# Sparse attention into a swish block on one core: key tiles moved by 16 tokens, attention tiled by head pair, long-run float32 loads, crossbar transposes, the first batch in halves, and every engine in written order

## The chip, the core and the metric

The kernel runs on one core of a Trainium2 chip (trn2). The engines are named as the profile names them: PE multiplies matrices (PEld is its weight load), DVE and ACT work on vectors, POOL does so too and issues its own DMAs, and SP only issues DMAs and waits. The metric is the time of one execution in device microseconds (us); lower is better. Several executions are timed, and one more is profiled.

## The reference

For each of 4 batches and 8 heads (768 tokens, head width 64) the kernel computes attention over two kinds of keys, and the result of all heads goes through a two-layer block.

```python
k_sum = k.reshape(B, H, nb, block, D).max(axis=3)      # 24 blocks of 32 tokens
v_sum = v.reshape(B, H, nb, block, D).mean(axis=3)
scores_l = scale * q @ k^T, kept where |i - j| < 16    # else -1e9
scores_s = scale * q @ k_sum^T + log(block)
a = softmax(concat(scores_l, scores_s))
attn = a @ concat(v, v_sum)
x = attn as (B*S, H*D)                                 # 3072 x 512
h = x @ w_in                                           # 512 x 2048
g = h * sigmoid(beta * h)
out = g @ w_out                                        # 2048 x 512
```

Inputs and output are float32. Both kernels multiply in bfloat16 and accumulate in float32.

## The kernel before

**Attention.** A query tile has 64 tokens, so a sequence has 12 of them. A query tile needs the keys from 15 tokens before it to 15 after it, and the 24 block maxima. Keys and queries of two heads (a pair, `g`, four per batch) lie on 128 partitions, 64 per head. One key tile of 128 columns holds 64 + 32 keys, 24 block maxima and padding. Even and odd query tiles (`par`) have different layouts: `kw` has a copy for each. A query operand `q2` holds the two heads side by side with zeros in the other head's rows, so that one matmul of 128 rows and 128 columns gives the scores of both heads (`scores`, L244, matmuls L259). ACT takes the exponential (L261). In batch 0 the mask is added by a matmul (L254); in the others DVE multiplies by a band of zeros and ones (L264). `av` (L267) multiplies by values that carry a column of ones, so that the sum of the weights comes out as well (L276); DVE takes the reciprocal (L278) and scales (L281).

**Preparation.** POOL loads and casts keys, queries and values (`load` L76, `casts` L184). PE transposes keys and queries (`prep_qk` L208, matmuls L215 and L235), DVE and ACT copy them out of PSUM. `prep_v` (L191) forms the block means by six matmuls, and four small SP transfers place value rows and means. `x_transpose` (L286) turns the attention result on PE. In batch 0 the loads are float32 and go through SP's and ACT's queues; later ones go through POOL's queue and are cast on the way.

**The block.** `h_tile` (L301) makes 128 of the 2048 hidden rows for 768 tokens: eight matmuls of 384 columns into one PSUM tile of two banks, and one ACT instruction on both banks (L309). `o_part` (L314) makes a fourth of one 128-token output block: four matmuls of 512 columns; after the fourth part DVE copies the block to SBUF (L324) and SP stores it (L325). Two output blocks share one PSUM tile, a bank each; the pool has three such tiles, and scores, attention results, hidden rows and outputs draw from it in turn.

**Order.** `merge` (L327) interleaves the preparation of the next batch with the `h_tile`s of this one, and the next batch's scores and `av`s with this batch's `o_part`s. SP and POOL run in written order (L25); PE, DVE and ACT are ordered by the scheduler of the language. The weights are loaded by POOL's queue, `w_in` and `w_out` in four pieces each (L342, L345), behind the casts of batch 0. `w_out` is divided by `beta` in place (L170).

Of the kernel before, what the change touches and what calls it, by code (L numbers as in the profile page):

```python
# [11 lines left out]
def kernel(  # L13
# [11 lines left out]
    ctx.enter_context(tc.manual_schedule(engines={mybir.EngineType.SP, mybir.EngineType.Pool}))  # L25
# [4 lines left out]
    ACTF = mybir.ActivationFunctionType  # L30

# [5 lines left out]
    nch = S // P  # L37
    NE = 2
    NF = S // NE
    nc3 = NF // P  # L40
    npair = H // 2
# [4 lines left out]
    n_tokens = B * S  # L46
    k1 = d_model // P
    k2 = d_ff // P
    VW = 2 * D + 1
    NEG = -30000.0  # L50


    SUM = (QT + W, W)
    assert d_model == H * D and out.shape == (n_tokens, d_model)

    const = ctx.enter_context(tc.tile_pool(name="consts", bufs=1))
    wpool = ctx.enter_context(tc.tile_pool(name="weights", bufs=1))
    qk_pool = ctx.enter_context(tc.tile_pool(name="qk", bufs=4))
    st_pool = ctx.enter_context(tc.tile_pool(name="st", bufs=9))
    at_pool = ctx.enter_context(tc.tile_pool(name="attn", bufs=4))  # L60
    x_pool = ctx.enter_context(tc.tile_pool(name="x", bufs=3))
    xt_pool = ctx.enter_context(tc.tile_pool(name="xt", bufs=2))
    moe_pool = ctx.enter_context(tc.tile_pool(name="moe", bufs=2))
    ps = ctx.enter_context(tc.tile_pool(name="ps", bufs=1, space=bass.MemoryType.PSUM))

    q_r, k_r = (a.rearrange("b (g h) (c p e) d -> b g p (h c) (e d)", p=P, h=2, e=NE) for a in (q, k))
    v_r = v.rearrange("b (g h) (c p) d -> b g p (h c) d", p=P, h=2)
    out_r = out.rearrange("(a p) d -> a p d", p=P)
    srcs = {"v": v_r, "k": k_r, "q": q_r}
    FE = 2 * S * D // P  # L70


    staged = {}
    hold = [moe_pool.tile([P, 4, FE], f32, name=f"hold{i}", tag="h_sb", bufs=4) for i in range(3)]

    def load(nm, b, g, eng):  # L76
        if b == 0:
            i = ("k", "q", "v").index(nm)
            f = hold[i][:, g]
        else:  # L80
            f = st_pool.tile([P, FE], bf16, name="st", tag="st")[:]
        dst = f.rearrange("p (n d) -> p n d", d=D if nm == "v" else NE * D)
        eng.dma_start(out=dst, in_=srcs[nm][b, g])  # L83
        staged[(nm, b, g)] = f

    load("k", 0, 0, nc.sync)
    load("q", 0, 0, nc.scalar)
    load("v", 0, 0, nc.sync)
    load("k", 0, 1, nc.scalar)
    load("q", 0, 1, nc.sync)  # L90
    load("v", 0, 1, nc.scalar)


    identity = const.tile([P, P], bf16, name="identity")
    make_identity(nc, identity)
    identity32 = const.tile([P, P], f32, name="identity32")
    nc.vector.tensor_copy(out=identity32[:], in_=identity[:])
# [5 lines left out]
    A_avg = const.tile([P, nch, P], bf16, name="A_avg")  # L103
    nc.vector.memset(A_avg, 0.0)
    nc.vector.memset(A_avg[:, :, 0:nb], 1.0 / block)
    select(A_avg[:, :, 0:nb], 0, [[P, nch], [-block, nb]], 1)
    select(A_avg[:, :, 0:nb], block - 1, [[-P, nch], [block, nb]], -1)

    band = const.tile([P, 2, QT], bf16, name="band")
    negband = const.tile([P, 2, QT], bf16, name="negband")  # L110
    bias = const.tile([P, 2], f32, name="bias")
    for par in range(2):
        near, far, summ = (const.tile([P, QT], bf16, name=f"{nm}{par}") for nm in ("near", "far", "summ"))
        nc.vector.memset(near, 1.0)
        nc.vector.memset(far, 1.0)
        nc.vector.memset(summ, 1.0)
        o = QT * par
        select(near, W - 1 - o, [[-1, QT]], 1)
        select(near, W - 1 + o, [[1, QT]], -1)
        if par == 0:  # L120
            select(far, -(P - W) - 1, [[-1, QT]], 1)
        else:
            select(far, -(QT - W) - 1, [[1, QT]], -1)
        select(summ, -SUM[par], [[0, QT]], 1)
        select(summ, SUM[par] + nb - 1, [[0, QT]], -1)
        nc.vector.tensor_add(out=near, in0=near, in1=far)

        nc.vector.tensor_add(out=band[:, par], in0=near, in1=summ)
        nc.vector.tensor_scalar(out=negband[:, par], in0=band[:, par], scalar1=1.0, scalar2=-NEG,  # L129
                                op0=ALU.subtract, op1=ALU.mult)  # L130
        nc.vector.tensor_scalar(out=bias[:, par:par + 1], in0=summ[:, 0:1], scalar1=log_block,
                                scalar2=None, op0=ALU.mult)

    NKW = 4
    kw_bufs = [const.tile([P, 2, nch, P], bf16, name=f"kw{i}") for i in range(NKW)]
    q2_bufs = [const.tile([P, nch, 2, 2, QT], bf16, name=f"q2{i}") for i in range(NKW)]

    ve_bufs = [const.tile([P, npair, nch + 1, VW], bf16, name=f"ve{i}") for i in range(2)]
    vo_bufs = [const.tile([P, npair, nch + 1, VW], bf16, name=f"vo{i}") for i in range(2)]

    def clear_qk(i):
        nc.vector.memset(q2_bufs[i][0:D, :, :, 1, :], 0.0)
        nc.vector.memset(q2_bufs[i][D:P, :, :, 0, :], 0.0)
        for par in range(2):
            nc.vector.memset(kw_bufs[i][:, par, :, SUM[par] + nb:SUM[par] + 2 * W], 0.0)
        nc.vector.memset(kw_bufs[i][:, 0, 0, P - W:P], 0.0)
        nc.vector.memset(kw_bufs[i][:, 1, nch - 1, 0:W], 0.0)

    def clear_v(i):
        nc.vector.memset(ve_bufs[i][:, :, 0:nch, 2 * D:VW], 1.0)  # L150
        nc.vector.memset(ve_bufs[i][:, :, nch], 0.0)
        nc.vector.memset(vo_bufs[i][:, :, 1:, 2 * D:VW], 1.0)
        nc.vector.memset(vo_bufs[i][:, :, 0], 0.0)

    clear_qk(0)
    clear_v(0)

    w_in_sb = wpool.tile([P, k1, d_ff], bf16, name="w_in_sb")
    w_out_sb = wpool.tile([P, k2, d_model], bf16, name="w_out_sb")
    beta_sb = wpool.tile([P, k2], f32, name="beta_sb")  # L160
    inv_beta = wpool.tile([P, k2], f32, name="inv_beta")
    beta_tmp = wpool.tile([k2, P], f32, name="beta_tmp")

    def load_beta():
        beta_ps = ps.tile([P, k2], f32, name="beta_ps", tag="t", bufs=2)
        nc.tensor.transpose(beta_ps[:], beta_tmp[:], identity32[:k2, :k2])
        nc.vector.tensor_copy(out=beta_sb[:], in_=beta_ps[:])
        nc.vector.reciprocal(out=inv_beta[:], in_=beta_sb[:])

    def scale_w_out(n):  # L170
        nc.vector.tensor_scalar(out=w_out_sb[:, n], in0=w_out_sb[:, n], scalar1=inv_beta[:, n:n + 1],
                                scalar2=None, op0=ALU.mult)

    last = {}

    def cast_qk(nm, b, g):
        t = qk_pool.tile([P, nc3, NE, 2, D], bf16, name=nm + "_nat", tag=nm + "_nat")
        f = staged.pop((nm, b, g)).rearrange("p (h c e d) -> p c e h d", h=2, e=NE, d=D)
        last["cast"] = nc.gpsimd.tensor_copy(out=t[:], in_=f)  # L179
        return t  # L180
# [3 lines left out]
    def casts(b, g):  # L184
        nat[(b, g)] = cast_qk("k", b, g), cast_qk("q", b, g)
        ve, vo = ve_bufs[b % 2][:, g], vo_bufs[b % 2][:, g]
        f = staged.pop(("v", b, g)).rearrange("p (h c d) -> p c h d", h=2, d=D)
        nc.gpsimd.tensor_copy(out=ve[:, 0:nch, 0:2 * D].rearrange("p c (h d) -> p c h d", h=2), in_=f)
        nc.gpsimd.tensor_copy(out=vo[:, 1:, 0:2 * D].rearrange("p c (h d) -> p c h d", h=2), in_=f)

    def prep_v(b, g):  # L191
        ve, vo = ve_bufs[b % 2][:, g], vo_bufs[b % 2][:, g]
        vm_ps = ps.tile([P, 2 * D], f32, name="vm_ps", tag="t", bufs=2)
        for c in range(nch):
            nc.tensor.matmul(vm_ps[:], A_avg[:, c, :], ve[:, c, 0:2 * D], start=(c == 0), stop=(c == nch - 1))  # L195
        vm = x_pool.tile([nb, 2 * D], bf16, name="vm", tag="vm")
        nc.vector.tensor_copy(out=vm[:], in_=vm_ps[0:nb])
        nc.sync.dma_start(out=vo[0:W, 1:], in_=ve[0:W, 1:])
        nc.sync.dma_start(out=ve[P - W:P, 0:nch], in_=vo[P - W:P, 0:nch])
        src = vm[:, None].to_broadcast([nb, nch, 2 * D])  # L200
        nc.sync.dma_start(out=ve[SUM[0]:SUM[0] + nb, 0:nch, 0:2 * D], in_=src)
        nc.sync.dma_start(out=vo[SUM[1]:SUM[1] + nb, 1:, 0:2 * D], in_=src)

    xT = {}
    x_nat = {}
    at = {}

# [157 lines left out]
    for g in range(npair):  # L365
        casts(0, g)
        if g == 2:
            load_w_in(0)
# [87 lines left out]
```

## Time and profile before

| | us |
|---|---|
| three timed executions | 260.85, 263.31, 315.06 (median 263.31) |
| span of the profiled execution, first to last instruction | 261.8 |
| PE busy in the span | 228.0 (87%) |
| DVE, ACT, POOL busy | 153.3, 115.6, 93.3 |
| hidden rows, 512 matmuls of 384 columns | 91.1 busy |
| outputs, 384 matmuls of 512 columns | 92.0 busy |
| exponentials and hidden-row activations on ACT | 28.2 and 57.5 |
| first hidden-row matmul; first unbroken stretch of them | at 43.8; from 50.6 |
| batch starts after it, by the chain | 103.6, 157.7, 211.7 |

The profile's page is that of one execution. No separate time of that execution is listed: its span is 1.5 us below the median of the timed ones. A row of a group reads: line, engine, operation, what is written from what is read, shape and count, then busy time, the mean time of one in ns, and the idle time before. Busy time of PE counts the overlap of matmuls that follow each other once, while the mean of one includes its way through the array: matmuls of 384 columns take 333 ns each by the row, and 16 of them in a row pass in 2.60 us, 162 ns each.

### The profile page before, as it was taken

What the parts mean: (1) busy time and instruction counts of PE and PEld (TensorE: products, weight loads), DVE (VectorE), ACT (ScalarE), POOL (GpSimd) and SP (SyncE); (2) the same over time, 40 slices, a digit from 0 to 9 for tenths busy, and PEclk for the clock granted to TensorE, in tenths of its full rate; (3) what the DMA queues carried; (4) which work ended last, traced back from release to release, by engine and by line L of the source; (5) the groups of instructions that cost most, each with busy time, mean ns of one, the idle gap of its engine ahead of it and who ended that gap; (6) DMA issues with size and microseconds to landing.
All of it is one profiled execution on the core that took longest, in us unless ns stands there. A gap on an engine that the chain in (4) does not pass through costs nothing.

```text
span 261.8 us, 4353 instructions
## 1 busy us (share of the span) xinstructions
PE 228.0 (87%) x1681; PEld 138.1 (53%) x1681; DVE 153.3 (59%) x355; ACT 115.6 (44%) x136; POOL 93.3 (36%) x126
## 2 busy tenths in 40 slices
PE   0473866599999879999999999999999999999984
PEld 0262643266665545566665555666655545654431
DVE  7672775669668888266658792666688831001221
ACT  1355641376684320476782331677833306661000
POOL 6679522599999990199510000000000000000000
PEclk9997695789999999999999999999999999999999
DMA  7999999999899999279401111101011111001111
GB/s 180 264 262 148 192 206 201 163 106 112 88 141 148 119 112 155 82 72 119 49 18 74 49 40 62 31 24 25 21 40 71 52 43 40 0 0 43 73 54 73
DMA packets 63667, 24.53 MB, mean 94 GB/s; under 512 B 49808, under 2 KB 60576, under 8 KB 63648
## 3 DMA queue, kind: packets, MB, share of 16 engines
q0 software_dynamic: 41664, 11.28, 42.8%
q1 hardware_dynamic: 18864, 11.82, 16.6%
q10 hardware_dynamic: 3120, 1.18, 2.0%
q8 instruction: 13, 0.21, 0.3%
q14 instruction: 6, 0.05, 0.1%
HBM read 27.27 MB, written 6.29 MB: 128 GB/s over the span
## 4 chain that ended last, share of the span: by engine, by line
PE 68%; DMA 12%; DVE 9%; POOL 5%; SPq 2%; issue 2%; ACT 1%; POOLq 0%; ACTq 0%
PE h_ps L307 32%; PE o_ps L320 25%; DMA st<-in_k_dram 8%; DVE x_nat L281 4%; DMA hold_86<-in_v_dram 4%; DVE attn L264 3%; PE s_ps L259 2%; SPq L83 2%; PE px L292 2%; PE av_ps L276 2%; PE pk L215 2%; PE vm_ps L195 2%; PE pq L235 2%; ACT attn L261 1%; POOL w_in_sb L343 1%
## 5 line engine op out<-in xcount | busy, mean ns | idle before, releaser
L320 PE MATMUL o_ps<-w_out_sb,h_sb 128*128 128x512 bf16 x384 | 92.0, 379 | 0.8 <-DVE o_sb L324 0.8
L307 PE MATMUL h_ps<-xT,w_in_sb 128*128 128x384 bf16 x512 | 91.1, 333 | 0.0
L309 ACT ACTIVATE h_sb<-h_ps,beta_sb 128x768 bf16<-128x768 f32 x64 | 57.5, 900 | 49.8 <-PE h_ps L307 48.9
L307 PEld LDWEIGHTS <-w_in_sb 128*128 128x128 bf16 x512 | 49.8, 99 | 31.6 <-issue 2.0
L320 PEld LDWEIGHTS <-h_sb 128*128 128x128 bf16 x384 | 35.9, 98 | 35.1 <-issue 1.5
L324 DVE COPY o_sb<-o_ps 128x512 f32<-128x512 f32 x24 | 16.6, 690 | 48.7 <-PE o_ps L320 48.4
L261 ACT ACTIVATE attn<-s_ps,bias 128x768 bf16<-128x768 f32 x32 | 28.2, 900 | 34.7 <-PE s_ps L259 26.9
L281 DVE TENSOR_TENSOR x_nat<-av_ps,r 64x384 bf16<-64x384 f32 x64 | 35.5, 555 | 1.5
L276 PEld LDWEIGHTS <-attn 128*128 128x128 bf16 x192 | 14.2, 103 | 16.9 <-issue 6.2
L264 DVE TENSOR_TENSOR attn<-attn,band 128x768 bf16<-128x768 bf16 x24 | 16.1, 671 | 9.9 <-ACT attn L261 9.6
L179 POOL COPY k_nat<-st 128x768 bf16<-128x768 bf16 x12 | 10.9, 908 | 21.5 <-PE pk L215 16.4
L227 DVE TENSOR_REDUCE km<-pk 128x24 bf16<-128x768 bf16 x16 | 15.2, 950 | 5.2 <-ACT kw_139 L225 1.7
L83 POOL DMA_DIRECT2D st<-in_v_dram x12 | 12.5, 1040 | 5.5 <-DMA w_in_sb<-in_moe_w_in_dram 3.2
L215 PEld LDWEIGHTS <-k_nat 128*128 128x128 bf16 x96 | 7.7, 110 | 11.1 <-issue 6.0
L254 PE MATMUL s_ps<-negband,identity 128*128 128x384 bf16 x16 | 6.5, 422 | 7.2 <-DVE negband L129 7.0
L276 PE MATMUL av_ps<-ve_146,attn 128*128 128x129 bf16 x48 | 4.9, 242 | 9.0 <-DMA ve_146<-vm 9.0
L278 DVE RECIPROCAL r<-av_ps 128x6 f32<-128x6 f32 x32 | 6.2, 194 | 10.9 <-PE av_ps L276 10.4
L215 PE MATMUL pk<-identity,k_nat 128*128 128x128 bf16 x96 | 9.3, 239 | 3.1 <-POOL k_nat L179 3.1
L292 PE MATMUL px<-identity,x_nat 128*128 128x128 bf16 x96 | 8.8, 232 | 3.3 <-DVE x_nat L281 2.9
L83 POOL DMA_DIRECT2D st<-in_q_dram x12 | 10.0, 837 | 2.7 <-DMA w_out_sb<-in_moe_w_out_dram 1.8
L235 PE MATMUL pq<-identity,q_nat 128*128 128x128 bf16 x96 | 9.0, 236 | 2.2 <-POOL q_nat L179 1.7
L292 PEld LDWEIGHTS <-x_nat 128*128 128x128 bf16 x96 | 5.9, 103 | 9.4 <-DVE x_nat L281 9.4
(136 smaller groups left out, 240.9 us busy)
## 6 DMA issues: line engine op xcount, KB each, us to landing
out_dram<-o_sb SPq DMA_DIRECT2D x24, 256.0 KB
st<-in_k_dram POOLq DMA_DIRECT2D x12, 192.0 KB, 3.9
st<-in_q_dram POOLq DMA_DIRECT2D x12, 192.0 KB, 4.9
st<-in_v_dram POOLq DMA_DIRECT2D x12, 192.0 KB, 5.7
w_in_sb<-in_moe_w_in_dram POOLq DMA_DIRECT2D x4, 512.0 KB, 8.2
w_out_sb<-in_moe_w_out_dram POOLq DMA_DIRECT2D x4, 512.0 KB, 17.5
hold_84<-in_k_dram SPq DMA_DIRECT2D x3, 384.0 KB
hold_86<-in_v_dram SPq DMA_DIRECT2D x3, 384.0 KB
```

The lines of the kernel that those rows point to most:

```text
L83: eng.dma_start(out=dst, in_=srcs[nm][b, g])
L215: nc.tensor.transpose(pk[:, e, c * P:(c + 1) * P], kt[:, c, e], identity)
L227: nc.vector.tensor_reduce(out=km[:], in_=pk.rearrange("p e (n f) -> p n e f", f=block // NE), op=ALU.max, axis=mybir.AxisListType.XY)
L261: nc.scalar.activation(out=a.rearrange("p (k j) h q -> p k (j h q)", k=2), in_=big[:, :, 0:w], func=ACTF.Exp, bias=bias[:, par:par + 1], s ...
L264: nc.vector.tensor_mul(out=a, in0=a, in1=band[:, par, None, None, :].to_broadcast([P, nch, 2, QT]))
L276: nc.tensor.matmul(ov[:, m // TB, m % TB], a[:, m], vt[:, m], start=True, stop=True)
L281: last["norm"] = nc.vector.tensor_mul(out=x[par * QT:(par + 1) * QT, :, hh, :].rearrange("p (k j) d -> p k j d", k=2), in0=ov[lo:lo + D, : ...
L292: nc.tensor.transpose(px[:, c * P:(c + 1) * P], x[:, c], identity)
L307: nc.tensor.matmul(big[:, kk, 0:MG], w_in_sb[:, ki, ni * P:(ni + 1) * P], xT[b][:, ki, kk * MG:(kk + 1) * MG], start=(ki == 0), stop=(ki = ...
L309: nc.scalar.activation(out=h_bufs[(b, ni // 8)][:, ni % 8, :].rearrange("p (k m) -> p k m", k=2), in_=big[:, :, 0:MG], func=ACTF.Silu, sca ...
L320: nc.tensor.matmul(o_ps, h_bufs[(b, ni // 8)][:, ni % 8, ms * P:(ms + 1) * P], w_out_sb[:, ni, :], start=(ni == 0), stop=(ni == k2 - 1))
L324: nc.vector.tensor_copy(out=o_sb[:], in_=o_ps)
```

## The change

Nearly every line of the kernel is written anew. Names and lines from here on are the new ones where they differ.

- **All engines in written order.** The scheduler places nothing any more; `run` and `put` write each side task behind a numbered main task. Four PSUM tiles of two banks each (`big[0]` to `big[3]`) are named by hand and stay for the whole kernel.
- **Key tiles moved by 16 tokens.** One layout for all 12 query tiles: 96 keys, 24 maxima, 8 zeros. The values get the matching layout: the tile `ve` starts 16 tokens early and has 13 tiles for two heads, `vo` is `ve` moved by 64 rows. The mask is the same for every tile but the first and last.
- **Attention per head and pair.** A scores matmul has 64 rows (one head) and 64 columns; the two heads use the two halves of the array's rows and the two banks of a tile. In `av` the weights are the 64 columns of one query tile, 65 value columns pass, and the result lands in one half of the partitions. DVE scales both heads of a pair in one instruction.
- **Loads.** Keys and queries come as float32 in runs of 2 KB (1 KB for the first batch's queries, which come in halves) on 96 partitions, values in runs of 256 bytes. All go through SP's queue. `w_in` stays on POOL's queue; `w_out` comes as float32 through SP's queue in eight pieces and is cast and divided by `beta` on DVE.
- **Transposes.** In batch 0 keys and queries are transposed on PE in float32 by matmuls with an identity (`kt0`, `qt0`), the attention result on PE in bfloat16. In batches 1 to 3 all three are transposed by DMAs on SP's queue (`kq_dma`, `x_dma`), after a cast on DVE (keys) or POOL (queries).
- **Batch 0 in halves.** Scores, `av` and the result are made for tokens 0 to 383 first and then for 384 to 767; the hidden rows likewise, in two passes of 16 `h_half`s, each followed by its own ACT instruction.
- **Outputs.** `o_atom` puts all output blocks of a batch into `big[0]`, the banks in turn; the first three blocks of batch 0 run side by side (`o3`), the last block of all is cut in two.

The core of the new code:

```diff
-    ctx.enter_context(tc.manual_schedule(engines={mybir.EngineType.SP, mybir.EngineType.Pool}))
+    ctx.enter_context(tc.manual_schedule())
+    big = [ps.tile([P, 2, 512], f32, name=f"big{i}") for i in range(4)]
...
+    def kt0(g):
+        t = big[g % 2].rearrange("p k (c f) -> p (k c) f", f=P)[:, :, 0:R]
+        f = stg[("k", 0, g)][0:R].rearrange("p (h c d) -> p h c d", h=2, d=D)
+        for c in range(8):
+            for h in range(2):
+                nc.tensor.matmul(t[h * D:(h + 1) * D, c], f[:, h, c], identity32[0:R, 0:R], start=True, stop=True)
+        windows(act_cp, g, t)
+        key_max(g, t)
+        key_sums(nc.gpsimd, g)
...
+        for j in range(HT):
+            m = u * HT + j
+            for h in range(2):
+                lo = h * D
+                nc.tensor.matmul(s[:, h, j * QT:(j + 1) * QT], kw[g][lo:lo + D, m, :], q_tile(b, g, h, m),
+                                 start=not on_pe, stop=not on_pe or j == HT - 1)
...
+    def v_odd_dma(g):
+        nc.sync.dma_start(out=vo[0:QT, g, :, :], in_=ve[QT:P, g, :, :])
+        nc.sync.dma_start(out=vo[QT:NK, g, 0:JV - 1, :], in_=ve[0:2 * W, g, 1:JV, :])
...
+    def vm_all(bg, bank):
+        t = big[bg][:, bank].rearrange("p (h g d) -> p h g d", h=2, g=G)
+        for h in range(2):
+            for j in range(J6 + 1):
+                nc.tensor.matmul(t[:, h], A[:, j], ve[:, :, h * J6 + j, 0:D], start=(j == 0), stop=(j == J6))
+        r = slice(NK, NK + nb)
+        nc.vector.tensor_copy(out=vm_sb[r], in_=t[r])
...
+                    nc.tensor.matmul(tv[par * QT:(par + 1) * QT, j, h], e[:, h, lo:lo + QT],
+                                     (vo if par else ve)[:, g, h * J6 + J, 0:D + 1], start=True, stop=True)
...
+    def x_dma(b, g):
+        nc.sync.dma_start_transpose(out=xT[:, g, :].rearrange("p (j t) -> p j t", j=J6),
+                                    in_=xn[(b, g)].rearrange("p j h d -> p (j h d)"))
...
+    def kq_dma(nm, b, g):
+        t = (kT if nm == "k" else qT)[g]
+        nc.sync.dma_start_transpose(out=t[:], in_=nat[(nm, b, g)][0:R].rearrange("p c h d -> p (c h d)"))
...
+    def h_half(i, kk, t):
+        lo = kk * HS
+        for ki in range(k1):
+            nc.tensor.matmul(t[:, 0:HS], w_in_sb[:, ki, i * P:(i + 1) * P], xT[:, ki, lo:lo + HS],
+                             start=(ki == 0), stop=(ki == k1 - 1))
+        nc.scalar.activation(out=h_sb[:, i, lo:lo + HS], in_=t[:, 0:HS], func=ACTF.Silu, scale=beta_sb[:, i:i + 1])
...
+    def o_atom(b, ms, a):
+        t = big[0][:, ms % 2]
+        for n in range(4 * a, 4 * a + 4):
+            o_mm(ms, n, t)
+        if a == 3:
+            o_out(b, ms, t)
...
+    banks = [big[3][:, 0], big[3][:, 1], big[0][:, 0], big[0][:, 1], big[1][:, 0], big[1][:, 1]]
...
+    run([lambda i=i: h_half(i, 0, banks[i % 6]) for i in range(k2)], sides)
...
+            put(sides, 0, lambda n=n: [load_k(n, g, nc.sync) for g in range(G)],
+                lambda n=n: [load_q(n, g, nc.sync) for g in range(G)])
+            for g in range(G):
+                put(sides, 2 + g, lambda g=g: kq_cast(nc.vector, "k", n, g), lambda g=g: kq_dma("k", n, g))
+            put(sides, 5, lambda n=n: [load_v(n, g, nc.sync) for g in range(G)])
+            for g in range(G):
+                put(sides, 4 + g, lambda g=g: windows(pool_cp, g, kT[g][:]), lambda g=g: key_max(g, kT[g][:]),
+                    lambda g=g: key_sums(nc.vector, g))
+                put(sides, 6 + g, lambda g=g: kq_cast(nc.gpsimd, "q", n, g), lambda g=g: kq_dma("q", n, g))
+                put(sides, 11 + g, lambda g=g: v_cast(nc.gpsimd, g), lambda g=g: v_odd_dma(g))
+            put(sides, 15, lambda: vm_all(3, 0))
+        run([lambda i=i: h_tile(i) for i in range(k2)], sides)
+        sides = {}
+        if n < B:
+            attention(n, sides, [0, 1, 4, 5, 6, 7, 8, 9], 7, 2, None)
+            put(sides, 2, lambda: vm_spread(nc.vector, vo), lambda: vm_spread(nc.vector, ve))
+        main = [lambda ms=ms, a=a: o_atom(b, ms, a) for ms in range(J6 - (n == B)) for a in range(4)]
+        run(main, sides)
```

`windows` copies the 96 keys of each of the 12 tiles into `kw` (three copies), `key_max` takes the 24 maxima, `key_sums` writes them into the tiles, `v_cast` casts values into `ve`, `vm_spread` copies the block means into `ve` or `vo` (two copies each), and `attention` writes the scores and `av`s of the next batch behind the numbered output parts. `qt0` is `kt0` for four of eight columns of the queries, with one copy out of PSUM by DVE.

## The prediction

> **What bounds the kernel now.** I read the page's busy rows and slices first, then the chain in order of time, then the groups for durations.
>
> ```profile
> PE 228.0 (87%) x1681; PEld 138.1 (53%) x1681; DVE 153.3 (59%) x355; ACT 115.6 (44%) x136; POOL 93.3 (36%) x126
> PE   0473866599999879999999999999999999999984
> PE 68%; DMA 12%; DVE 9%; POOL 5%; SPq 2%; issue 2%; ACT 1%; POOLq 0%; ACTq 0%
> ```
>
> PE is full from slice 8 on (6.5 us each) and leads the chain: after the first 50 us the kernel is a queue of matmuls. The chain in order of time shows what one costs:
>
> ```profile
> 109.95 0.34 PE pq L235 x6
> 110.28 2.60 PE h_ps L307 x16
> 112.88 0.35 PE vm_ps L195 x6
> 236.08 17.44 PE o_ps L320 x80
> 253.54 0.70 DVE o_sb L324
> 254.29 3.63 PE o_ps L320 x16
> ```
>
> A matmul of 384 columns passes in 2.60/16 = 0.162 us, one of 512 in 17.44/80 = 0.216 (218 by the row), one of 128 with its own weights in 0.34/6 = 0.057. So the block costs 512 x 0.162 + 384 x 0.216 = 166 us in any order. The last three lines show a price that the change pays often: the sixth output block uses the other bank of the PSUM tile that the fifth has just filled, and PE stands from 253.54 to 254.29, until DVE has copied the first bank. Elsewhere the scheduler puts other matmuls there (the page gives L320 0.8 us of idle in all).
>
> ```profile
> L309 ACT ACTIVATE h_sb<-h_ps,beta_sb 128x768 bf16<-128x768 f32 x64 | 57.5, 900 | 49.8 <-PE h_ps L307 48.9
> L179 POOL COPY k_nat<-st 128x768 bf16<-128x768 bf16 x12 | 10.9, 908 | 21.5 <-PE pk L215 16.4
> st<-in_k_dram POOLq DMA_DIRECT2D x12, 192.0 KB, 3.9
> ```
>
> These give ACT's time for two banks, POOL's for 768 elements (829 to 908 ns, 1.1 ns an element), and 3.9 us from issue to landing for a pair's keys. By form:
>
> ```profile
> L166 PE MATMUL beta_ps<-identity_98,beta_tmp 16*128 16x16 f32 x1 | 0.2, 231 | 0.0
> L230 DVE COPY kw_139<-km 128x144 bf16<-128x144 bf16 x8 | 4.1, 599 | 0.1
> L230 DVE COPY kw_141<-km 128x144 bf16<-128x144 bf16 x8 | 1.4, 223 | 0.1
> ```
>
> **What the change does to PE's work.** Before, 768 short matmuls: 192 scores, 192 `av`, 288 transposes, 96 for block means. After, 384 scores and 384 `av`: 768 again, with 64 or 65 columns instead of 128. A weight load still stands before each, so I price them at 0.055, near the 0.057 row. Bounds: 0.028 (half the columns), 0.1 (the 97 to 109 ns of a weight load, unhidden). So crossbar transposes take 4 us a batch off PE and finer attention puts 5 us on. No gain here.
>
> [...]
>
> **Same-tile waits.** In the built program the first matmul into the second bank of a tile waits for the reader of the first. `h_half` fills a bank with four matmuls (0.65), ACT reads it, and only then comes the other bank: ACT's 384 columns take about 0.55 (between half of 0.900 and 0.6), with 0.17 to leave the array (333 less 162 ns) and 0.08 of signals 0.8. Nothing can fill the gap, since the order is written. `o_atom` uses `big[0]` for all blocks, so each block pays what 253.54 to 254.29 shows, with the drain 0.95.
>
> **Stage by stage**, following each engine's written order with these durations:
>
> *Until the first hidden-row matmul: 51* (before 43.8, and 50.6 until unbroken). The first keys land near 3.5 (first long load before: 5.07 - 0.81 with two queues sharing). Then PE runs all 128 float32 transposes, since the second halves of queries and scores stand ahead of the first `h_half` too. The nearest float32 row is 231 ns at 16 columns; the nearest transposes take 57. I take 0.2, so 25.6. Scores and masks 7.4, `av` and means 4. POOL's chain of a pair (cast 0.9, four moves 1.1, weight issue 0.8) is 2.8 us against 1.4 of PE work, leaving 7 uncovered over four pairs; one PSUM bank waits for DVE's copies, 3. Sum 51; bounds 39 (0.057) and 58 (0.231, slow clock at the start). The halves thus bring little: only the second `av`s lie beside hidden rows.
>
> *Two passes of `h_half`: 43.* Each 16 x 0.65 = 10.4 and 8 x 0.8 = 6.4; the first also has four `av`s with their waits for DVE (4 x 1.1) and ACT's table load of 1.3 (sum 22); the second ends 4 us early for the weights (21).
>
> *Why the weights are late.* SP's order is keys, queries, four key transposes, one query transpose, then half of `w_out`. The key casts stand on DVE behind the first pass, and each next cast behind the maximum of the keys just transposed. A crossbar transpose is in no row: between 1.95 (an output store, issue to landing) and 5.7 (the value loads of the page); I take 3.5, near the keys' 3.9. A link is cast 0.9, transpose 3.5, maximum 0.95: 5.4, and four end when the second pass does. The eight `w_out` loads follow, then the values.
>
> *Outputs of batch 0: 47.* 20.7 + 192 x 0.055 = 10.6 + means 1.5, and waits: weights 4 + 4 + 2, two boundaries 2, `av` behind DVE's spread and scaling 5 (sum 50; I take 47, since the last waits overlap). Before: 28.
>
> *Hidden rows of batches 1 and 2: 31 each* (before, with preparation, 28). 20.8, the 14 matmuls of `vm_all` 3 (256 columns each, at half speed, as the trace's six L276 matmuls at 40.95 take 0.81 after a stall and 0.35 otherwise), and a stall of 7 at them. They need all four value casts, which stand on POOL behind four `windows` (1120 elements, 1.4 us) and four query casts (1.15): 5.5 + 4.6 + 3.7 = 14 us that begin only when the first keys are transposed, 10 us in, because that transpose stands on SP behind eight loads of 384 KB.
>
> *Outputs of batches 1 and 2: 40 each* (before 26). 20.7 + 10.6, then DVE's four `vm_spread` copies of 1536 elements ahead of the first output copy: at 0.9 each (the 144 broadcast elements of L230 in 223 ns give up to 2.4 if time goes by elements, and at least 0.22) and the mask products beside them 5 us of stall; two open boundaries 2, other waits 1.7.
>
> *Batch 3: 20.8 + 27.* 20.7, four boundaries 3.8, last copy and store 2.5.
>
> 51 + 43 + 47 + 31 + 40 + 31 + 40 + 48 = 331. This is against the profiled span of 261.8; the median of the timed runs is 1.5 above it, which I leave in the rounding: **330**.
>
> [...]
>
> **Rivals.**
>
> 1. *PE never waits* (the other side; place: both banks' borders, output borders, means). If hidden and output rows of the two banks flow without the waits and preparation is always ahead, the stalls above go: 13 in `h_half`, 16 + 8 + 8 + 4 at outputs, 7 + 7 at the means, 10 in the head: 73 less, 257, 2% under the time before. For: DVE at 59% and ACT at 44% have room. Against: the waits are in the program, and one stands in this trace at 253.54. It decides from 68 of the 73 on. Chance 0.04.
> 2. *Cheap transposes and short matmuls.* Float32 at 0.057 and short ones at 0.028: 12 less in the head, 15 in three output stages: 300 to 310. For: two heads use different rows of the array. Against: separate weight loads. Chance 0.22.
> 3. *The crossbar is the bound.* At 5.7 us or more a transpose, four links of the key chain add 9, each hidden stage 3, the borders of batches 3: 350 to 368. [...] Against: 192 KB is what one of the page's loads moves. Chance 0.24.
> 4. *The first batch is not in halves in effect*: counted above, since the halves do not shorten the head. Were all its second-half work to slide beside the first pass, the head would be 15 shorter: 315. It lies inside the forecast's band.
>
> Forecast 330 (312 to 348): chance 0.5.
>
> **Range.** The unknown prices give 300 (float32 0.057, short 0.028, transposes 1.95) to 368 (5.7, spread copies at 2.4); I leave 0.1 on each side: 300 to 368. A run can tell 2% from no change. Slower by over 2%: 0.96; within: 0.02; faster: 0.02, from rival 1, which lies on the border.
>
> **What would show it.** PE idle before `h_half` released by ACT, 16 times some 0.8; before `o_atom` released by DVE's output copy; before `vm_all` by POOL's value casts; the first output rows by the weights' scaling on DVE; the first hidden matmul near 51; periods of some 71 us instead of 54. Wrong if hidden rows begin under 40, the periods are under 62, or the transposes take over 6 us each.

## The result and the profile after

The changed kernel takes **340.62 us** (median of four executions, 337.52 to 341.82), the kernel before 263.26 beside it. The ratio is 1.294, 95% interval 1.283 to 1.305; here and below a ratio leaves out executions over 1.5% above the fastest of their kernel (of the kernel before the one at 315.06), a median does not, and none is given where a single execution would be left. In a later group the changed kernel took 340.89 (337.34 to 343.17). The profiled execution took 341.82, its span is 339.8.

First the page of the changed kernel: busy rows, slices (8.5 us each), granted clock, and the shares of the chain that ended last.

```profile
PE 254.5 (75%) x2057; PEld 141.6 (42%) x2075; DVE 129.3 (38%) x223; ACT 109.7 (32%) x144; POOL 73.0 (21%) x113
PE   4685677866386797599566997997046997999885
PEclk9995587999785799989858799999559899999999
PE 48%; DMA 18%; DVE 15%; ACT 7%; SPq 6%; issue 4%; POOL 2%; POOLq 0%; DVEq 0%; ACTq 0%
```

No engine but PE is busy for half the span, and PE is not full either. Its idle time is 339.8 - 254.5 = 85.3 us, against 261.8 - 228.0 = 33.8 before: 51.5 of the 78 us. The other 26.5 are more busy time. Of that, 6.5 is the output matmuls, the same work at a lower granted clock (0.85 to 0.91 in the outputs of batches 0 to 2, where the kernel before had 0.97 to 1.00 from 50.6 on; 98.5 us busy against 92.0; 18 of its 400 records are missing here, and the second profile of the changed kernel, which has them all, gives 101.7). The hidden rows took 64.9 + 25.5 = 90.4 against 91.1. The rest of PE's work, attention and transposes, went from 228.0 - 92.0 - 91.1 = 44.9 to 254.5 - 98.5 - 90.4 = 65.6; a part of that, some 8 us by an estimate from starts, is changes between matmuls that use different rows or columns of the array (last section).

Now the same execution cut at the first matmul of each stage. Columns: stretch, its length, busy time of PE, PEld, DVE, ACT and POOL with instructions, PE's granted clock, DMA share and GB/s.

```profile
0.00:48.70 48.70, 32.95 (x485) 25.61 (x485) 22.10 (x67) 15.71 (x28) 20.85 (x53) 0.79 0.94 199
48.70:92.70 44.00, 27.87 (x197) 13.99 (x189) 17.01 (x31) 21.12 (x36) 14.02 (x16) 0.92 0.23 59
92.70:139.00 46.30, 37.15 (x296) 18.20 (x303) 22.34 (x41) 9.87 (x11) 4.39 (x5) 0.85 0.64 167
139.00:175.90 36.90, 25.91 (x144) 15.08 (x143) 16.46 (x13) 14.42 (x16) 16.93 (x20) 0.84 0.90 193
175.90:214.60 38.70, 32.85 (x285) 15.57 (x289) 14.99 (x26) 9.87 (x11) 0.00 (x0) 0.89 0.26 64
214.60:253.40 38.80, 23.86 (x143) 14.52 (x142) 16.37 (x13) 14.42 (x16) 16.83 (x20) 0.82 0.90 177
253.40:290.70 37.30, 31.62 (x285) 15.33 (x288) 14.98 (x26) 9.87 (x11) 0.00 (x0) 0.91 0.31 67
290.70:311.50 20.80, 20.80 (x129) 12.53 (x128) 0.69 (x1) 13.52 (x15) 0.00 (x0) 1.00 0.04 13
311.50:339.80 28.30, 21.50 (x112) 10.81 (x111) 4.31 (x7) 0.90 (x1) 0.00 (x0) 0.97 0.15 56
```

Every stage that prepares a next batch is long and at a clock of 0.82 to 0.92; the last batch has nothing to prepare and runs at 0.97 to 1.00. Set beside the kernel before, by its batch starts:

| from, to | before, us | after, us |
|---|---|---|
| start to the hidden rows of batch 1 | 103.6 | 139.0 |
| batch 1 | 54.1 | 75.6 |
| batch 2 | 54.0 | 76.1 |
| batch 3 | 50.1 | 49.1 |

Where PE stands is told by the view of waits, PE's rows of the changed kernel. Columns: who waits for whom, us in total, how often, the longest.

```profile
PE big L310 <- POOL ve L278: 22.3, 2, 14.9
PE big L390 <- DVE o_sb L395: 12.8, 12, 2.9
PE big L390 <- DVE w_out_sb L193: 10.6, 3, 5.1
PE big L373 <- ACT h_sb L375: 10.4, 16, 2.3
PE big L233 <- DMA stg<-in_k_dram: 4.5, 1, 4.5
```

The first four rows are 56 us: block means waiting for value casts, outputs for the copy of the block before or for scaled weights, half rows for ACT. PE's timeline shows the two same-tile waits (columns: start, length, what, and in brackets the idle time before it and its releaser):

```profile
71.83 1.46 PE L373 MATMUL big<-xT,w_in_sb 128*128 128x384 bf16 x8 [0.67 <-ACT h_sb L375]
...
320.39 3.61 PE L390 MATMUL big<-w_out_sb,h_sb 128*128 128x512 bf16 x16 [0.78 <-DVE o_sb L395]
```

Eight matmuls, two half rows, then 0.67 of nothing; and 0.78 between two output blocks of the last batch.

The chain in order of time, ahead of the block means of batch 3, shows how the longest kind of wait comes about:

```profile
216.36 4.36 DMA stg<-in_k_dram
220.72 12.74 DMA kT<-kn
...
248.78 1.66 POOL ve L278 x2
...
250.49 3.14 PE big L310 x14
```

The first key transpose is issued at 220.72 and lands 12.74 later, at 233.45: it stands behind eight loads of 384 KB. POOL copies keys from there on without a break, value casts last, and PE's means begin at 250.49.

### The profile page after: what moved, and what is told of

The parts are those of the page before. It is cut to its first block, busy times and chain, and to the rows that moved or that the text cites. A ratio compares the mean times of both kernels' runs of the same rounds, so it can differ in the third digit from the quotient of the medians.

```text
span 339.8 us, 5101 instructions
## 1 busy us (share of the span) xinstructions
PE 254.5 (75%) x2057; PEld 141.6 (42%) x2075; DVE 129.3 (38%) x223; ACT 109.7 (32%) x144; POOL 73.0 (21%) x113
## 4 chain that ended last, share of the span: by engine, by line
PE 48%; DMA 18%; DVE 15%; ACT 7%; SPq 6%; issue 4%; POOL 2%; POOLq 0%; DVEq 0%; ACTq 0%
PE big L390 24%; DMA kT<-kn 9%; PE big L383 6%; PE big L267 5%; ACT e L271 3%; PE big L373 3%; DVE o_sb L395 3%; DMA stg<-in_k_dram 3%; DMA vst<-in_v_dram 3%; DVE km L213 2%; PE big L243 2%; PE big L310 2%; PE big L332 2%; DMA beta_tmp<-in_moe_beta_dram 2%; DVE xn L343 2%
## 5 line engine op out<-in xcount | busy, mean ns | idle before, releaser
L390 PE MATMUL big<-w_out_sb,h_sb 128*128 128x512 bf16 (+1 forms) x382 | 98.5, 400 | 26.4 <-DVE o_sb L395 12.8
L390 PEld LDWEIGHTS <-h_sb 128*128 128x128 bf16 x400 | 39.2, 103 | 72.2 <-issue 35.9
L383 PE MATMUL big<-xT,w_in_sb 128*128 128x384 bf16 x384 | 64.9, 332 | 3.7 <-DMA xT<-xn 3.7
L385 ACT ACTIVATE h_sb<-big,beta_sb 128x768 bf16<-128x768 f32 x48 | 43.2, 901 | 67.0 <-PE big L383 67.0
L226 POOL COPY kw<-kT 128x80 bf16<-128x80 bf16 (+1 forms) x36 | 30.2, 880 | 140.8 <-DMA kT<-kn 135.3
L271 ACT ACTIVATE e<-big,bias 128x768 bf16<-128x768 f32 x32 | 28.4, 901 | 50.7 <-PE big L267 50.7
L373 PE MATMUL big<-xT,w_in_sb 128*128 128x384 bf16 x128 | 25.5, 338 | 10.4 <-ACT h_sb L375 10.4
L273 DVE TENSOR_TENSOR e<-e,mask 128x768 bf16<-128x768 bf16 x24 | 13.4, 558 | 43.9 <-ACT e L271 43.8
L213 DVE TENSOR_REDUCE km<-kT 128x24 bf16<-128x768 bf16 x12 | 17.5, 1455 | 27.6 <-DMA kT<-kn 27.6
L310 PE MATMUL big<-ve,A_avg 128*128 128x256 bf16 x42 | 8.0, 367 | 22.3 <-POOL ve L278 22.3
L375 ACT ACTIVATE h_sb<-big,beta_sb 128x384 bf16<-128x384 f32 x32 | 18.6, 581 | 18.3 <-PE big L373 17.6
L267 PE MATMUL big<-qT,kw 64*128 64x64 bf16 x288 | 19.6, 281 | 0.0
L217 DVE COPY kw<-km 128x288 bf16<-128x288 bf16 x12 | 16.8, 1401 | 0.4
L343 DVE TENSOR_TENSOR xn<-big,r 128x768 bf16<-128x768 f32 (+1 forms) x20 | 15.9, 797 | 0.7
L310 PEld LDWEIGHTS <-A_avg 128*128 128x128 bf16 x42 | 5.3, 126 | 24.8 <-issue 22.7
```

The costliest lines, as they stand in the source:

```text
L213: nc.vector.tensor_reduce(out=km[g][:], in_=src.rearrange("p c (n f) -> p n f c", f=4), op=ALU.max, axis=AX.XY)
L226: nc.gpsimd.tensor_copy(out=o, in_=i)
L267: nc.tensor.matmul(s[:, h, j * QT:(j + 1) * QT], kw[g][lo:lo + D, m, :], q_tile(b, g, h, m), start=not on_pe, stop=not on_pe or j == HT - 1)
L271: nc.scalar.activation(out=e[:], in_=s[:, :, 0:HS], func=ACTF.Exp, bias=bias[:, 0:1], scale=scale)
L310: nc.tensor.matmul(t[:, h], A[:, j], ve[:, :, h * J6 + j, 0:D], start=(j == 0), stop=(j == J6))
L343: nc.vector.tensor_mul(out=x[:, 3 * us[0]:3 * us[0] + 3 * n].rearrange("p (k j) h d -> p k (j h) d", k=n), in0=tv[:, :, :, 0:D], in1=r[:, ...
```

## The experiments

Each edit starts from the changed kernel. Medians are of four executions; the kernel before, on the same chips, was at 262.6 to 263.8. The changed kernel's eight executions span 337.3 to 343.2, so a few us are not resolved by the medians alone, and I read single edits by their stages too.

| run | median, us (range) | ratio to before, 95% |
|---|---|---|
| changed kernel again | 340.89 (337.34 to 343.17) | 1.275 to 1.298 |
| bank order | 332.83 (331.39 to 336.02) | 1.258 to 1.278 |
| output tiles | 330.99 (327.51 to 334.76) | 1.237 to 1.260 |
| late query loads | 330.02 (326.53 to 330.91) | 1.241 to 1.265 |
| late means | 333.98 (333.82 to 334.13) | 1.267 to 1.278 |
| early key casts | 332.86 (328.89 to 336.63) | 1.247 to 1.268 |
| beta first | 338.88 (330.66 to 341.46) | |
| transposes twice | 397.72 (396.32 to 397.92) | 1.507 to 1.521 |
| transposes twice, spare tile | 352.58 (351.97 to 354.64) | 1.328 to 1.348 |
| scheduler | 303.37 (296.68 to 304.74) | |
| hand edits together | 299.93 (299.19 to 301.29) | 1.129 to 1.144 |
| hand edits and scheduler | 289.18 (287.40 to 289.86) | 1.087 to 1.102 |

### The changed kernel once more

> The changed kernel once more, beside the others of this group, as the measure of what a few us mean. Expected 338 to 342 as before; if it lies near 331 to 334, the single edits that measured 330 to 334 are not told apart from no change.

340.89. The single edits at 330 to 334 are told apart from it. Its stages agree with those of the first profile within 0.6 us, but for the hidden rows of batch 2 (36.1 instead of 38.8): such a difference between two profiles is no effect of an edit.

### Bank order

```diff
-    banks = [big[3][:, 0], big[3][:, 1], big[0][:, 0], big[0][:, 1], big[1][:, 0], big[1][:, 1]]
+    banks = [big[3][:, 0], big[0][:, 0], big[1][:, 0], big[3][:, 1], big[0][:, 1], big[1][:, 1]]
```

> The six banks of the `h_half` passes are taken in another order, so that neighbours lie in different PSUM tiles. Theory (same-tile wait): the 16 waits of 0.65 us for ACT, 10.4 us in the profile of the change, go; 330 us if the weights of the outputs come earlier with the passes, 335 if the second pass only waits for them instead. Rival (ACT is the bound of the passes, 0.58 us per half against 0.65 of matmuls): the idle time stays under another name, 340.

332.83, between the two cases named. PE's waits of this run:

```profile
PE big L390 <- DVE w_out_sb L193: 18.5, 4, 12.2
...
PE big L373 <- ACT h_sb L375: 1.7, 2, 1.0
```

The waits for ACT fell from 10.4 to 1.7, so they were same-tile waits and ACT was not the bound. In exchange PE waits 18.5 for scaled weights instead of 10.6. The two passes are 38.9 long instead of 44.0, the outputs behind them 45.2 instead of 46.3; the rest of the 8 us is no more than two profiles of one kernel differ by.

Same tile, other bank: 0.67 us of idle. The changed kernel did take its banks in turn and had no overlap between the two of one tile; it came with another tile. In this program, which waits by tile, taking the banks in turn was not enough.

### Output tiles

```diff
-        t = big[0][:, ms % 2]
+        t = big[ms % 2][:, 0]
...
-            put(sides, s0[i], lambda g=g, u=u, i=i: scores(b, g, u, (2, 1)[i % 2]))
+            put(sides, s0[i], lambda g=g, u=u, i=i: scores(b, g, u, 2))
...
-            t = big[0 if lo else 3][:, 1]
+            t = big[2 if lo else 3][:, 1]
```

> Output blocks alternate between two PSUM tiles instead of two banks of one; the scores then have one tile instead of two. Theory (boundary wait): five boundaries of 0.75 us in the last batch go, -3 to -4, and of the other 9 us of waits for the output copy in batches 0 to 2 about half: 331 to 334. Rival (in batches 0 to 2 DVE is late with the copy anyway, and the scores now wait for ACT): only the last batch gains, 336 to 338.

330.99, at the theory's lower end. By stages: outputs of batch 1 from 38.7 to 34.2, of batch 2 from 37.3 to 33.8, of batch 3, from its first matmul to its last, from 24.8 to 20.9. There nothing but the boundaries was changed. In batch 0 the stage is 2.8 longer: the scores now wait for ACT there (4.8 us in three waits, the longest 2.3). So the boundary cost 0.8 each, and the scores' second tile was worth something too.

### Late query loads

```diff
             put(sides, 0, lambda n=n: [load_k(n, g, nc.sync) for g in range(G)],
-                lambda n=n: [load_q(n, g, nc.sync) for g in range(G)])
+                )
             for g in range(G):
-                put(sides, 2 + g, lambda g=g: kq_cast(nc.vector, "k", n, g), lambda g=g: kq_dma("k", n, g))
+                put(sides, 2 + g, lambda g=g: kq_cast(nc.vector, "k", n, g), lambda g=g: kq_dma("k", n, g),
+                    lambda n=n, g=g: load_q(n, g, nc.sync))
```

> In batches 1 and 2 the loads of the next queries are put behind the key transposes on SP. Theory (SP's queue holds the keys back): the first transposed keys land 4 x 1.7 = 7 us earlier, the two waits of PE for the value casts (22.3 us) shrink by 7 each, 326 to 328. Rival (POOL's chain of windows, query casts and value casts sets the end, and its query casts now start late): -3 to +2, 337 to 342.

330.02 against 326 to 328. The hidden rows of batch 1 went from 36.9 to 31.0, of batch 2 from 38.8 (36.1 in the second profile) to 32.4, and the wait from 22.3 to

```profile
PE big L310 <- POOL ve L278: 11.2, 2, 8.5
```

The place in SP's queue held the keys back, by 5.5 us a batch.

### Late means

```diff
-            put(sides, 15, lambda: vm_all(3, 0))
...
-            put(sides, 2, lambda: vm_spread(nc.vector, vo), lambda: vm_spread(nc.vector, ve))
+            put(sides, 2, lambda: vm_all(3, 0), lambda: vm_spread(nc.vector, vo), lambda: vm_spread(nc.vector, ve))
```

> The means of the next batch stand three output parts later instead of before the last hidden tile's end. Theory (PE only waits there because the means stand too early): the 14.9 and 7.4 us of waiting shrink by the 4 us of output and score matmuls that now come first, 332 to 334. Rival (the scores of the next batch or the spread copies are late next, so that the wait only changes its name): 338 to 342.

333.98, the theory's number, but not its mechanism:

```profile
PE big L267 <- DMA qT<-qn: 15.1, 2, 8.5
```

The wait for value casts is gone and PE waits 15.1 us for the next queries. The hidden rows got 10.5 and 15.3 us shorter (36.9 to 26.4, 36.1 to 20.8 against the second profile), the outputs after them 7.1 and 11.5 longer. Most of the wait changed its name: preparation as a whole is late, not the means.

### Beta first

The load of `beta` is moved ahead of the loads of batch 0's keys.

> The load of beta is the first in SP's queue instead of the ninth. Theory: PE's 2.7 us behind that load in the head goes, and the float32 transposes then run at about 0.1 us each, so the first hidden rows come 2 to 3 us earlier: 338. Rival (the head is set by POOL's value casts or by the loads of the keys and queries): 340 to 341.

Not settled by the times: the four executions lie between 330.7 and 341.5. In the profile the wait of 2.7 us is gone and the first hidden row starts at 43.8 instead of 48.7 and 49.3; with all hand edits it starts at 44.1. That is more than the wait, which was 2.7 in the first profile of the changed kernel and 4.1 in the second. For the rest the record shows only a granted clock of 0.78 from 36 to 44 us, where the changed kernel had 0.50 in both profiles; no run tells which way cause and effect go.

### Transposes twice

```diff
-        nc.sync.dma_start_transpose(out=t[:], in_=nat[(nm, b, g)][0:R].rearrange("p c h d -> p (c h d)"))
+        for _ in range(2):
+            nc.sync.dma_start_transpose(out=t[:], in_=nat[(nm, b, g)][0:R].rearrange("p c h d -> p (c h d)"))
```

> Every transpose of keys and queries by DMA is issued twice, 24 more of 192 KB. Theory (a transpose costs its turn in SP's queue, 1.25 us, and lies in the chains of the keys): batch 1's key chain ends 5 to 11 us later and the value casts of batches 2 and 3 up to 5 each: 348 to 360. Rival (the crossbar itself is the bound): 24 x 2.75 = 66 more, 400. Rival (all transposes lie under other work): 340 to 342.

397.72: my theory failed and the rival's number came. But the waits of SP's queue in this run (L368 is the transpose) say why:

```profile
SPq L368 <- DMA kT<-kn: 31.0, 12, 8.2
...
SPq L368 <- DMA qT<-qn: 24.4, 12, 5.1
```

The second transpose writes the tile of the first, so SP waited 24 times until it had landed, 55.4 us in all, and 57 came on top of the time. The run doesn't tell the crossbar from the wait, so the second transpose was given a tile of its own:

```diff
-        nc.sync.dma_start_transpose(out=t[:], in_=nat[(nm, b, g)][0:R].rearrange("p c h d -> p (c h d)"))
+        for o in (t, spare[g]):
+            nc.sync.dma_start_transpose(out=o[:], in_=nat[(nm, b, g)][0:R].rearrange("p c h d -> p (c h d)"))
```

> As the run with every key and query transpose issued twice, but the second one writes a spare tile that nobody reads, so that it doesn't wait for its twin to land. Theory (the turn in SP's queue is the cost, 1.25 us when nothing is waited for): 24 x 1.25 = 30 us more on SP, of which the first doubled run showed 57 of 67 in the time: 340 + 25 = 365, range 355 to 372. Rival (the crossbar or its buffers are the cost, 2.75 each): 398 again. Rival (the doubled run only paid for the waits of SP on its own twin in the key chains): 345 to 352.

352.58: 12 us for 24 transposes, 0.5 each, less than my 25, at the upper edge of the rival in which the doubled run had paid only for SP's waits (345 to 352), and far from the crossbar's 398. The crossbar is not the bound. A transpose is cheap where SP has time, and a wait on SP is dear, since everything behind it waits too: of the 57 us some 45 are left for the 55.4 us of waiting on SP, when the 12 of the transposes themselves are taken off.

### Early key casts

```diff
-        put(sides, 2 + 2 * g, lambda g=g: kq_cast(nc.vector, "k", 1, g), lambda g=g: kq_dma("k", 1, g))
+        put(sides, 2, lambda g=g: kq_cast(nc.vector, "k", 1, g), lambda g=g: kq_dma("k", 1, g))
```

> In batch 1 all four key casts and transposes come ahead of the first maximum of the keys. Theory (the chain cast, transpose, maximum, 5.6 us a link, holds the output weights back): the last keys are transposed 10 us or more earlier, the weights too, and PE's 10.6 us of waits for scaled weights fall under 3: 331 to 334. Rival (the weights wait for staging tiles that POOL's query casts free, or the values are late next): 337 to 341.

332.86, in the theory's range, by half its mechanism. The fourth key transpose landed at 77.55 instead of 87.93, and the passes are 39.5 long instead of 44.0. PE's waits for scaled weights are 6.1 though, not under 3, and what is left is not the loads. The second four were issued from 91.0 on and landed at 94.92, 96.35, 97.69 and 99.23, yet DVE scaled the first two of them from 99.92 on and the last two from 107.64 on. In DVE's written order mask products stand ahead, and these wait for ACT's exponentials. The changed kernel's timeline shows the same order, with two of the loads landed at 99.62 and 101.44:

```profile
103.50 0.56 DVE L273 TENSOR_TENSOR e<-e,mask 128x768 bf16<-128x768 bf16 x1 [0.23 <-ACT e L271]
103.98 1.67 DVE L193 TENSOR_SCALAR w_out_sb<-stg,inv_beta 128x512 bf16<-128x512 f32 x4
```

So the chain link was the cause of the first late weights, DVE's written order of the others. No run moves the scaling alone; in the scheduler's run below, no wait of PE for scaled weights is left.

### The scheduler

```diff
-    ctx.enter_context(tc.manual_schedule())
+    ctx.enter_context(tc.manual_schedule(engines={mybir.EngineType.SP, mybir.EngineType.Pool}))
```

> PE, DVE and ACT are ordered by the language's scheduler, as in the kernel before; SP and POOL stay in written order. Theory (the written order is why nothing fills the waits): part of the 50 us of waits on PE is filled, 315 to 330. Rival (the waits are for data that no order brings sooner, or the tiles named by hand leave the scheduler nothing to place): 338 to 350.

303.37: 37.5 us for one line by the medians, 40.7 between the fastest executions (296.68 and 337.34), more than the theory's 10 to 26 and about half of the loss. Tiles, loads and SP's order are the same, and so are the instructions but for three more table loads on ACT. The waits of half rows for ACT and of block means for value casts are gone; what stays is

```profile
L390 PE MATMUL big<-w_out_sb,h_sb 128*128 128x512 bf16 (+1 forms) x400 | 96.5, 393 | 20.5 <-DVE o_sb L395 20.2
```

the boundary, which goes with a second tile (next section).

### Hand edits together, then with the scheduler

The first has bank order, output tiles, late query loads, late means, beta first and early key casts in written order; the second is the same with the scheduler's line.

> All hand edits together, still in written order: bank order, output tiles, late query loads, late means, beta first, early key casts of batch 1. Theory (the waits are separate): the single gains of 8, 10, 10, 7, 2 and 8 us would sum to 45, of which the late query loads and the late means share one wait of 7: about 300, range 292 to 308. Rival (they mostly move one wait about): 315 to 325.

> The hand edits together, and PE, DVE and ACT ordered by the scheduler. Theory (scheduler and hand edits remove different waits: the scheduler's run still has 20 us of waits for output copies and 11 us each for the first transposed keys): 280 to 290. Rival (both remove the same waits, which are gone with the hand edits): as the hand edits alone, 295 to 305. The kernel before stays ahead of all of them at 263.

299.93 and 289.18, both in the theories' ranges: the gains nearly add up, and scheduler and hand edits each remove waits that the other leaves. The output matmuls' group in the second run's page:

```profile
L390 PE MATMUL big<-w_out_sb,h_sb 128*128 128x512 bf16 (+1 forms) x400 | 89.6, 375 | 0.1
```

PE has 73% of the chain, and the outputs wait for nothing any more. The span is 285.5 with PE busy 245.1: 40.4 us idle, 6.6 more than in the kernel before, and 17.1 more busy. Busy time more than waiting is then what keeps this version behind 263; of all versions the kernel before stays the fastest.

## Why the prediction was right

330 was said, with 300 to 368, and 340.6 came. The stages, in us:

| stage | said | profile |
|---|---|---|
| until the first hidden-row matmul | 51 | 48.7 |
| two passes of half rows | 43 | 44.0 |
| outputs of batch 0 | 47 | 46.3 |
| hidden rows of batch 1 | 31 | 36.9 |
| outputs of batch 1 | 40 | 38.7 |
| hidden rows of batch 2 | 31 | 38.8 |
| outputs of batch 2 | 40 | 37.3 |
| batch 3 | 47.8 | 49.1 |

**Same-tile waits**: shown. The idle time between two pairs of half rows was 0.67 where 0.8 was said, the output boundary 0.78 where 0.95 was said, of which 0.17 was for leaving the array. With another tile the waits for ACT fell from 10.4 to 1.7, and the boundary by 0.8.

**Late weights**: shown for the first of the three waits; that the sum agrees is in part luck. The sum had 10 us, all laid on late loads, the profile has 10.6. Of these the first wait, 5.1, is the loads'. The other two, 3.4 and 2.0, end with scaling that stood on DVE behind mask products (early key casts, above), a wait that the prediction didn't name. The chain of cast, transpose and maximum was priced at 5.4 a link; the four key transposes were issued at 68.42, 74.07, 79.64 and 85.18, 5.6 apart.

**Hidden rows of batches 1 and 2**: the mechanism was right, the size was not, and this is the step that was mis-sized, by 5.9 and 7.8 us (5.5 and 5.1 in the second profile). "Begin only when the first keys are transposed, 10 us in", said the prediction of POOL's chain: they were transposed at 155.83 and 233.45, 17 and 19 us in. The eight loads landed 1.6 us apart (219.97 the first, 231.25 the last), and the transpose behind them. POOL's chain, said to take 14, took 16.8 (233.60 to 250.44), as the copies of `windows` came to 2.6 a pair instead of 1.4:

```profile
L226 POOL COPY kw<-kT 128x960 bf16<-128x960 bf16 x12 | 21.7, 1808 | 140.8 <-DMA kT<-kn 135.3 <-PE big L373 2.8 <-ACT h_sb L375 2.7
L226 POOL COPY kw<-kT 128x80 bf16<-128x80 bf16 x24 | 9.3, 415 | 0.0
```

The price was some 1.2 ns an element, from casts of whole rows of 64; these copies take their elements 96 apart and cost 2.4 each (2.64 us for 1120). That the distance is the reason was not tested.

**Short matmuls**: said 0.055 each. Twelve scores passed in 0.77 (0.064 each), 24 `av` matmuls in 0.57 (0.024): 0.044 on the mean, 8 us less in all.

**Float32 transposes**: said 0.2, so 25.6. The two groups (128 transposes, two records each) are 9.7 + 9.0 = 18.7 busy, 0.146 each. The head did not get that much shorter, since PE also waited 4.5 for keys and 2.7 for `beta`, which the sum didn't have.

**Crossbar transposes**: said 3.5 from issue to landing. Unhindered they took 2.85 (68.42 to 71.27), each with 1.2 of SP. Behind other transfers two landed 0.7 apart (96.49, 97.18). "Over 6 us each" was named as a sign of being wrong, and behind the eight loads the first took 12.7; the spare tile's run shows that this was the place in the queue.

**Spread copies**: said 0.9 each, measured 0.55; with the cheaper `av`, outputs of batches 1 and 2 came 1.3 and 2.7 under the forecast.

**The rivals.** That PE never waits fell with the first profile. Cheap transposes and short matmuls was half right in its prices and didn't decide, since the hidden rows grew by more. The crossbar as the bound fell with the spare tile. Halves without effect holds: the second halves' scores and float32 transposes stand ahead of the first half row, as said. That is the written order's doing: the scheduler starts the first half row at 39.2 instead of 48.7.

What the forecast had no term for is the clock: PE is granted 0.82 to 0.92 in the stages with waits and 0.97 to 1.00 in the last batch. Four output matmuls at 184.99, after a wait of 2.86, took 1.87 us at a granted clock of 0.50, and 1.04 at 196.56 at a clock of 1.00; the output matmuls alone show 6.5 us of that. That the waits bring the low clock about is not tested apart from them; where the outputs wait for nothing (hand edits with the scheduler) they take 89.6. Nor did the sum have a term for changes between matmuls that use different rows or columns of the array: some 8 us, as the last section works out, part of them inside the prices of the short matmuls above.

## What to carry to other kernels

Before an order is written out by hand, ask for each wait on the busiest engine what stands behind it that could have run; here one line that gave the order back to the scheduler was worth 37 us of a loss of 77. A second bank of the same tile is no second buffer where waits go by tile (here 0.67 and 0.78 us of idle each time). A queue that serves loads, transposes and stores in one written order passes its waits on to what stands behind (here 55.4 us of waits on SP brought some 45 us of time): put the transfer that others need first, and count its position, not only its duration.

## What the runs showed of the hardware

**Two halves of the array at once.** An `av` matmul of the even tiles and one of the odd tiles, with different halves of the output partitions, start at the same time (timeline of the changed kernel):

```profile
60.77 0.19 PE L332 MATMUL big<-ve,e 128*64 128x65 bf16 x1
60.77 0.19 PE L332 MATMUL big<-vo,e 128*64 128x65 bf16 x1
```

I had priced them one after the other, at 0.055 each; 24 passed in 0.57 us, 0.024 each.

**Changes of the rows or columns in use took 0.1 us each.** Matmuls that use all of the array (128*128 in their rows) and matmuls that use a part of it (64*128, 128*64) follow each other often in the changed kernel. Idle time doesn't show a cost: the scores of batches 1 to 3, with 64 rows each, have 0.0 us before them by their row. But a matmul's idle time counts from the modelled end of the one before, 0.38 us after its start, and this covers what lies between the starts. The starts show it. Four output matmuls ahead of scores, from the chains of the kernel before and of the changed kernel, both at a granted clock of 1.00:

```profile
76.99 0.86 PE o_ps L320 x4
77.85 0.34 PE s_ps L259 x6
...
192.60 0.97 PE big L390 x4
193.57 0.76 PE big L267 x12
```

The four start some 0.22 apart in both. In the kernel before, where outputs and scores both use the whole array (128*128 in their rows), the first score starts 0.216 after the last of the four. In the changed kernel, where a score uses 64 rows (64*128), it starts 0.311 after it, 0.095 more. Most other changes that nothing else delays cost 0.09 to 0.11; what PE does in that time no run shows. The trace has 105 changes, 76 of them without idle time before them, which makes some 8 us, an estimate from these starts.

**DVE beside POOL.** The same DVE copy of 288 elements took between 0.52 and 5.09 us. The long one lies under an unbroken run of POOL copies and casts, from 155.98 to 172.91 (timeline, both engines):

```profile
162.04 2.34 POOL L226 COPY kw<-kT 128x960 bf16<-128x960 bf16 x3
162.10 5.09 DVE L217 COPY kw<-km 128x288 bf16<-128x288 bf16 x1
...
165.31 2.31 POOL L226 COPY kw<-kT 128x960 bf16<-128x960 bf16 x3
```

So does the scaling of the weights: 0.47 to 0.49 alone, 1.0 to 1.25 where POOL was casting. The 5.09 us are longer than any one of POOL's copies and casts beside it (1.82 at most): the copy lasted through several in a row. Lying beside POOL is not enough, however: the copies at 157.35 and 160.04, under the same run, took 0.54 and 0.63, and why is open. Here it cost little, since PE waited for POOL's casts and not for these copies; no run took POOL's work away to test it.
